# Three groups on each converted weight chunk, and a written engine order from group 3 on

## The chip, the cores and the metric

One core of a Trainium2 chip runs the whole program. The metric is device time in microseconds (us) of one execution. The five engines that matter are TensorE (PE; its weight loads are listed as PEld), VectorE (DVE), ScalarE (ACT), GpSimd (POOL) and SyncE (SP, which issues most DMAs).

## The reference

```python
def reference(q, k, v, moe_w_in, moe_w_out, ...):        # attention -> dense layer -> routed experts
    scores = q @ k.T / sqrt(64); mask 0 <= row - col < 128; bias -slope[h] * |row - col|
    attn = softmax(scores); x = attn @ v                 # 4 x 8 heads x 576 x 64 -> x: 2304 x 512
    h = max(x @ w_in, 0); x = (h * h) @ w_out            # 512 -> 2048 -> 512
    logits = x @ w_gate + log1p(exp(x @ w_noise)) * noise
    top2 of 8 experts, softmax weights of the two
    out = sum over both: weight * (max(x @ w1[e], 0) @ w2[e])    # 512 -> 1024 -> 512
```

The dense weights arrive as float64, everything else as float32.

## The kernel before

The 2304 tokens are 18 **tiles** `i` of 128. Attention is done by tile. The dense layer is done by 9 **groups** `g` of 256 tokens (tiles 2g and 2g+1) and 16 **chunks** `f` of 128 of the 2048 hidden columns. One pair (g, f) is called a **unit** here. Its matmuls are `mm1` (12 matmuls 128x256 into `h`, L128) and `mm2` (6 matmuls 128x512 into the two banks `y` of the group, L133); between them stand the gate steps: three ACT passes (ReLU, square, high part `gh`) and on DVE the low part `gl` (L345). `mm2` comes two units behind its `mm1`. Each value is carried as a high and a low float32r part, which is why there are three products for each.

A tile's attention on PE is: scores (L250, 12 matmuls for each half of the heads), transposes (L290), value products (L305). On DVE it is: `ktl` (L218), the masked merge (L255), bias and row maximum (L264), the small softmax steps (L267, L273, L274), the two masked copies of the transposed weights (L293, L294) and the low part `xl` of its output (L312). ACT does copies and exponentials, POOL the scaling by the row sum (L277) in the later tiles.

A float64 chunk is converted once, in two halves, by `load_w_moe` (L99 to L118): an ACT pass, the sign on POOL (L111), two bit operations and a subtraction on DVE (L112, L114, L117). The result lives in one of 16 slots: chunks 0 to 7 in `ring_a`, chunks 8 to 15 in `ring_b`, whose memory is that of the pool `at0`, the attention buffers of the first tiles. So no chunk from 8 on is finished before the tiles in `at0` are.

**First pass.** `FT = 4` tiles are in `at0`, and groups 0 and 1 share the chunks, group 1 four chunks behind (`LATE = 4`). Group 2 and the later ones then run one after another, all chunks being there. Beside the units of group g (g from 2) the attention of group g+1 is issued in pieces (`a_pair`), and the routing of group g-1 (`routes`: output transposes, gate matmuls L382 and L391, top two, ranks, table matmuls L486). Group 8 has no attention beside it; its units cover the first loads of expert weights, and the routing of group 7. Then come the eight experts.

The Tile scheduler decides the order of all instructions on each engine from the order of the calls, the dependences and its own costs. PSUM has eight banks: four `y`, two `t` (transposes, value products, later scores) and two `h`. The zero fill of the output (`out_dram<-ysb`, 4608 KB) and the constants of the routing (`consts_late`) are issued at the beginning of group 2.

Of the kernel before, what the change touches and what calls it, by code (L numbers as in the profile page):

```python
# [22 lines left out]
def kernel(  # L23
# [75 lines left out]
    def load_w_moe(f):  # L99
        w = slot()  # L100
        for u in range(2):
# [4 lines left out]
            a = s64.tile([P, DM], I32, name="wa", bufs=3)  # L106
# [4 lines left out]
            nc.gpsimd.tensor_scalar(hi.bitcast(F32), hi.bitcast(F32), 0.0, None, op0=OP.mult)  # L111
            nc.vector.scalar_tensor_tensor(out=lo, in0=lo, scalar=29, in1=hi,  # L112
# [44 lines left out]
    def consts_late():  # L157
# [3 lines left out]
        nc.gpsimd.iota(io128, pattern=[[1, P]], base=0, channel_multiplier=0,  # L161
                       allow_small_or_imprecise_dtypes=True)
# [24 lines left out]

    def T(shape, dt=F32):
        return psp.tile(shape, dt, name="t", bufs=2)
# [10 lines left out]
    QT, VT, SB, PT, QK = {}, {}, {}, {}, {}  # L200
# [13 lines left out]
    def a_qk(i, what="qk"):  # L214
        t = QK.pop(i)
# [3 lines left out]
        if "q" in what:  # L219
            qh = A["p"].tile([P, H // 2, P], F32R, name="qh", bufs=A["qt"])  # L220
            ql = A["p"].tile([P, H // 2, P], F32R, name="ql", bufs=A["qt"])
            eng = nc.vector if i < 1 else nc.gpsimd
            eng.tensor_tensor(out=t[:, 0], in0=t[:, 0], in1=qscale[:, :, None].to_broadcast([P, H // 2, P]),
                              op=OP.mult)
            nc.scalar.activation(qh, t[:, 0], AF.Copy)
            eng.tensor_tensor(out=ql, in0=t[:, 0], in1=qh.bitcast(F32), op=OP.subtract)
            QT[i] = (qh, ql)
# [11 lines left out]
    def a_s(i, hf):  # L239
# [4 lines left out]
        sp = [psp.tile([P, 2, 2, P], F32, name="y", bufs=4) if A["early"] else T([P, 2, 2, P]) for _ in range(2)]  # L244
        for pp in range(2):
            p = 2 * hf + pp
            for n, (a, b) in enumerate(((qh, kh), (qh, kl), (ql, kh))):
                for c in range(2):
                    r = slice(64 * c, 64 * c + 64)
                    nc.tensor.matmul(sp[c][:, pp], a[r, p, :], b[r, p, s0:s0 + 2, :], start=(n == 0), stop=(n == 2))  # L250
# [5 lines left out]
        mx = A["p"].tile([P, 4], F32, name="mx", bufs=A["sb"])  # L256
        nb = A["p"].tile([P, 4], F32, name="nb", bufs=A["sb"])
        sm = A["p"].tile([P, 4], F32, name="sm", bufs=A["sb"])
        rs = A["p"].tile([P, 4], F32, name="rs", bufs=A["sb"])
# [7 lines left out]
        nc.vector.tensor_tensor(out=nb, in0=mx, in1=nslope[:, 4 * hf:4 * hf + 4], op=OP.mult)  # L267
        for pp in range(2):
            for c in range(2):
                j = 2 * pp + c  # L270
                nc.scalar.activation(sb[:, c, pp], sb[:, c, pp], AF.Exp, bias=nb[:, j:j + 1],  # L271
                                     scale=2.0 ** -(4 * hf + j + 1), accum_out=sm[:, j:j + 1])
        nc.vector.tensor_scalar(sm, sm, 1e-9, None, op0=OP.add)  # L273
# [23 lines left out]
    def a_av(i, hf):  # L297
        o = T([P, 2, P])
        pts = PT.pop((i, hf))
        vv = (VT[max(i - 1, 0)], VT[i])  # L300
        for pp in range(2):
            for n in range(2):
# [10 lines left out]
        if hf == 1:  # L313
            VT.pop(i - 1, None)
# [547 lines left out]
```

## Time and profile before

| | us |
|---|---|
| median of 3 runs | 1071.94 (1069.54 to 1072.7) |
| profiled execution | 1073.84 (span 1072.1) |
| PE busy | 1014.4 (95%) |
| DVE busy | 569.1 (53%) |
| ACT busy | 507.7 (47%) |
| POOL busy | 245.2 (23%) |
| first mm1 of groups 2, 3 and 8 | 182.46, 247.99, 544.59 |
| first mm1 of expert 0 | 604.15 |

Spans are counted from the start of the profiled execution. The busy share is an average over stages with different limits, so the stages are read one by one. The profile also shows the granted clock of PE in each stretch (1.00 is full).

### The profile page before, as it was taken

The numbers are of one execution on the slowest core, as the hardware profiler recorded it, in microseconds if no ns is written. First come the engines' busy times: TensorE is split into PE (matmuls) and PEld (weight loads), VectorE is DVE, ScalarE is ACT, GpSimd is POOL, SyncE is SP. The second block draws the span as 40 slices with busy tenths as digits, with TensorE's granted clock in tenths as the row PEclk, the third lists the DMA queues.
The fourth block names the chain that finished last, engine by engine and source line by source line (L and its number), as shares of the span: only waits on it lengthen the run. The fifth ranks groups of instructions, "written<-read, shape, count | busy, mean of one in ns | idle before, by whom it ended". The sixth has DMA issues, their size and how long they took to land.

```text
span 1072.1 us, 17953 instructions
## 1 busy us (share of the span) xinstructions
PE 1014.4 (95%) x6636; PEld 876.9 (82%) x6636; DVE 569.1 (53%) x1700; ACT 507.7 (47%) x1272; POOL 245.2 (23%) x219
## 2 busy tenths in 40 slices
PE   4788899899999999999999899999999999999996
PEld 3567788788888888888887787988988888888885
DVE  7989873766555556465537455434443444342312
ACT  5876664665656465565557534332333232321110
POOL 2545530211101021111000012314141412232111
PEclk9989999999999999999999999999999999999998
DMA  6334412611101111110025506535353444432111
GB/s 235 118 126 152 149 59 85 236 31 50 31 30 31 35 46 31 40 41 20 12 91 159 175 27 186 166 113 177 98 164 108 159 124 138 132 105 71 45 46 47
DMA packets 36522, 104.19 MB, mean 97 GB/s; under 512 B 7527, under 2 KB 7783, under 8 KB 36432
## 3 DMA queue, kind: packets, MB, share of 16 engines
q1 hardware_dynamic: 27232, 75.72, 22.1%
q0 software_dynamic: 9200, 27.29, 8.1%
q8 instruction: 53, 0.87, 0.4%
q14 instruction: 37, 0.30, 0.1%
HBM read 86.02 MB, written 20.00 MB: 99 GB/s over the span
## 4 chain that ended last, share of the span: by engine, by line
PE 69%; DVE 9%; DMA 8%; issue 6%; ACT 6%; POOL 1%; SPq 0%; POOLq 0%; ACTq 0%; DVEq 0%
PE h L128 30%; PE y L133 27%; DMA old<-out_dram,idx 4%; PE t L133 3%; PE t L305 3%; PE y L250 2%; PE t L569 1%; PE t L290 1%; DMA qks<-in_qk_dram 1%; ACT sb L271 1%; DMA xg<-yd,idx 1%; DVE gl L345 1%; DVE sb L264 1%; DVE w L112 1%; POOL w L111 1%
## 5 line engine op out<-in xcount | busy, mean ns | idle before, releaser
L128 PE MATMUL h<-xh,w 128*128 128x256 f32 x1152 | 237.7, 289 | 5.3 <-ACT r L342 4.8
L128 PE MATMUL h<-xeh,w 128*128 128x304 f32 (+2 forms) x1024 | 229.5, 305 | 0.9 <-ACT xeh L572 0.9
L128 PEld LDWEIGHTS h<-xh,w 128*128 128x128 f32 x1152 | 190.7, 193 | 15.4 <-ACT r L342 6.6
L133 PE MATMUL y<-w,gh 128*128 128x512 f32 x576 | 189.0, 408 | 0.6 <-ACT gh L344 0.4
L128 PEld LDWEIGHTS h<-xeh,w 128*128 128x128 f32 x1024 | 171.4, 188 | 3.5 <-ACT xeh L572 1.1
L128 PE MATMUL h<-xl,w 128*128 128x256 f32 x576 | 164.8, 286 | 0.0
L96 DVE TENSOR_TENSOR w<-wst,w 128x1024 fp32r<-128x1024 f32 x64 | 78.4, 1226 | 148.5 <-ACT w L95 148.4
L128 PE MATMUL h<-xel,w 128*128 128x304 f32 (+2 forms) x512 | 154.8, 302 | 0.4 <-DVE wt L574 0.4
L133 PE MATMUL y<-w,hh 128*128 128x512 f32 x464 | 145.0, 393 | 0.0
L95 ACT ACTIVATE w<-wst 128x1024 fp32r<-128x1024 f32 x64 | 67.8, 1059 | 134.5 <-PE t L133 128.0
L588 ACT ACTIVATE hh<-h 128x304 fp32r<-128x304 f32 (+1 forms) x120 | 50.4, 420 | 147.6 <-PE h L128 146.1
L133 PE MATMUL y<-w,gl 128*128 128x512 f32 x288 | 114.3, 398 | 2.2 <-DVE gl L345 2.2
L133 PEld LDWEIGHTS y<-w,gh 128*128 128x128 f32 x576 | 99.1, 189 | 20.3 <-ACT r L343 1.0
L342 ACT ACTIVATE r<-h 128x256 f32<-128x256 f32 x144 | 54.4, 378 | 127.9 <-PE h L128 84.0
L128 PEld LDWEIGHTS h<-xl,w 128*128 128x128 f32 x576 | 111.0, 193 | 3.9 <-issue 0.3
L345 DVE TENSOR_TENSOR gl<-r,gh 128x256 fp32r<-128x256 f32 x144 | 66.5, 461 | 83.2 <-ACT gh L344 82.3
L589 DVE SCALAR_TENSOR_TENSOR hl<-h,hh 128x304 fp32r<-128x304 f32 (+1 forms) x120 | 55.9, 466 | 102.5 <-ACT hh L588 102.5
L541 POOL DMA_INDIRECT xg<-yd,idx x40 | 40.7, 1018 | 275.8 <-PE h L128 125.0
L128 PEld LDWEIGHTS h<-xel,w 128*128 128x128 f32 x512 | 96.4, 188 | 1.8 <-DVE wt L574 0.6
L133 PEld LDWEIGHTS y<-w,hh 128*128 128x128 f32 x464 | 83.9, 188 | 14.9
L277 POOL TENSOR_TENSOR sb<-sb,rs 128x512 f32<-128x512 f32 x28 | 29.8, 1064 | 273.9 <-ACT sb L253 130.4
L133 PE MATMUL y<-w,hl 128*128 128x512 f32 x232 | 91.2, 393 | 0.0
(190 smaller groups left out, 1620.9 us busy)
## 6 DMA issues: line engine op xcount, KB each, us to landing
wst<-in_w_exp_dram SPq DMA_DIRECT2D x64, 512.0 KB, 3.7
w<-in_w_moe_dram SPq DMA_DIRECT2D x32, 512.0 KB, 3.7
qks<-in_qk_dram SPq DMA_DIRECT2D x20, 512.0 KB, 3.7
vs<-in_v_dram SPq DMA_DIRECT2D x20, 256.0 KB, 2.7
yd<-ysb SPq DMA_DIRECT2D x18, 256.0 KB, 2.0
out_dram<-ysb SPq DMA_DIRECT2D x1, 4608.0 KB, 14.2
xg<-yd,idx POOLq DMA_INDIRECT x40, 3.7
out_dram<-old,idx POOLq DMA_INDIRECT x29, 2.8
```

The lines of the kernel that those rows point to most:

```text
L95: nc.scalar.activation(w[:, 0], st, AF.Copy)
L96: nc.vector.tensor_tensor(out=w[:, 1], in0=st, in1=w[:, 0].bitcast(F32), op=OP.subtract)
L128: nc.tensor.matmul(ps, w[:, wi, c], x[:, kk, :], start=(n == 0), stop=(n == 3 * KD - 1))
L133: nc.tensor.matmul(ps, g, w[:, wi, DM:], start=(start and n == 0), stop=(stop and n == 2))
L250: nc.tensor.matmul(sp[c][:, pp], a[r, p, :], b[r, p, s0:s0 + 2, :], start=(n == 0), stop=(n == 2))
L277: nc.gpsimd.tensor_tensor(out=sb, in0=sb, in1=r.to_broadcast([P, 2, 2, P]), op=OP.mult)
L305: nc.tensor.matmul(o[64 * c:64 * c + 64, pp, :], vv[n][:, 4 * hf + j, :], pts[n][:, j, :], start=(n == 0), stop=(n == 1))
L342: nc.scalar.activation(r, h, AF.Relu)
L345: nc.vector.tensor_tensor(out=gl, in0=r, in1=gh.bitcast(F32), op=OP.subtract)
L541: nc.gpsimd.indirect_dma_start(out=xg, out_offset=None, in_=yd[:rows, :], in_offset=col(e, t), bounds_check=rows - 1, oob_is_err=False)
L588: nc.scalar.activation(hh[:, c], ps, AF.Relu)
L589: nc.vector.scalar_tensor_tensor(out=hl[:, c], in0=ps, scalar=0.0, in1=hh[:, c].bitcast(F32), op0=OP.max, op1=OP.subtract)
```

## The change

1. First pass: `FT = 6` tiles in `at0`, and **three** groups on each chunk, starting at chunk steps 0, 3 and 6. `mm2` comes two units behind in the common order. Chunk 8 now waits for tile 5. The constants, the zero fill and the attention buffers of tiles 6 and 7 (`at2`) move to step 13; tiles 6 and 7 and the routing of groups 0 and 1 follow in steps 14 to 21.
2. From group 3 to group 7 the engines PE, ACT, DVE and POOL run in **the order of the calls** (`manual_schedule`). Each unit has a place, between its `mm1` and its gate steps, and a table (`a_places`, `r_places`) puts one step of attention or routing there. The scores of a tile are one block of both halves, its value products are one block in one PSUM bank (L339), its output copy is one pass of 512 columns (L352). What is left of the table (`rest`) goes into group 8.
3. PSUM: `t` is gone, and six banks `y` serve everything. `gh` and `gl` get three buffers each.
4. Conversion: the sign on POOL reads the contiguous ACT result `af` and writes a tile `sg` of its own; `wa` has two buffers instead of three.

```diff
-            a = s64.tile([P, DM], I32, name="wa", bufs=3)
+            a = s64.tile([P, DM], I32, name="wa", bufs=2)
+            sg = s64.tile([P, DM], I32, name="wsg", bufs=1)
-            nc.gpsimd.tensor_scalar(hi.bitcast(F32), hi.bitcast(F32), 0.0, None, op0=OP.mult)
-            nc.vector.scalar_tensor_tensor(out=lo, in0=lo, scalar=29, in1=hi,
+            nc.gpsimd.tensor_scalar(sg.bitcast(F32), af, 0.0, None, op0=OP.mult)
+            nc.vector.scalar_tensor_tensor(out=lo, in0=lo, scalar=29, in1=sg,
...
     def T(shape, dt=F32):
-        return psp.tile(shape, dt, name="t", bufs=2)
+        return psp.tile(shape, dt, name="y", bufs=6)
...
+    def a_places(i):
+        return [lambda: a_q1(i), lambda: (a_kq(i), load(i + 1, "qk")), lambda: a_s(i),
+                lambda: (a_cp(i, 0), a_cp(i, 1)), lambda: a_mx(i, 0), lambda: (a_ex(i, 0), a_mx(i, 1)),
+                lambda: (a_nm(i, 0), a_ex(i, 1)), lambda: (a_nm(i, 1), a_tp(i, 0)),
+                lambda: (a_m(i, 0), a_tp(i, 1)), lambda: (a_m(i, 1), a_av(i)), lambda: (a_x(i), load(i + 1, "v"))]
...
-    FT = 2 * GT
-    LATE = 4
-    NA = 3
+    FT = 3 * GT
+    LATE = (0, 3, 6)
+    NA = 6
...
-    for s in range(NFC + LATE):
-        now = [(g, s - LATE * g) for g in range(2) if 0 <= s - LATE * g < NFC]
-        for g, f in now:
-            m_mm1(g, f)
+    for s in range(NFC + LATE[-1]):
+        for g in range(len(LATE)):
+            f = s - LATE[g]
+            if not 0 <= f < NFC:
+                continue
+            m_h(g, f)
+            m_g(g, f)
+            prev.append((g, f))
+            while len(prev) > 2:
+                q = prev.pop(0)
+                m_mm2(*q)
+                if q[1] == NFC - 1:
+                    m_y(q[0])
+                    fill += routes(q[0])
+            for _ in range(2):
+                if s >= NFC and fill:
+                    fill.pop(0)()
...
+        if s + 3 == NFC:
             s64_cm.__exit__(None, None, None)
...
+    with tc.manual_schedule(engines=order):
+        for g in range(len(LATE), NG - 1):
+            for f in range(NFC):
+                m_h(g, f)
+                for fn in places.pop(NFC * g + f, ()):
+                    fn()
+                m_g(g, f)
+                prev.append((g, f))
+                m_mm2(*prev.pop(0))
+    rest = [fn for n in sorted(places) for fn in places[n]]
```

DVE at the end of the pool `at0`, which lets `ring_b` begin. `w`/`wa` are a chunk's buffers, `gl` is a gate's low part, `xl` a tile's output, and `wsg` the new sign tile. Before (tile 4's output comes among later chunks, long after `at0`):

```order
287 L345 TENSOR_TENSOR gl<-r,gh 128x256
288 L114 SCALAR_TENSOR_TENSOR wa<-wa,w_1526 128x512
289 L112 SCALAR_TENSOR_TENSOR w_1636<-w_1636 128x512
290 L117 TENSOR_TENSOR w<-wa,w 128x512
291 L114 SCALAR_TENSOR_TENSOR wa<-wa,w_1636 128x512
292 L312 TENSOR_TENSOR xl<-t,xh 128x2x128
293 L255 COPY_PREDICATED sb<-pmask,t 128x256
```

And of the change (the end of tile 5, and the first conversion into `ring_b` behind it):

```order
280 L325 TENSOR_TENSOR pv<-y,mprev 128x512
281 L326 TENSOR_TENSOR pc<-y,mcur 128x512
282 L385 TENSOR_TENSOR gl<-r,gh 128x256
283 L170 MEMSET ones 128x128
284 L171 MEMSET tab 128x152
285 L161 TENSOR_SCALAR tri<-io_2072 128x128
286 L168 TENSOR_SCALAR idx<-idx 128x16
287 L352 TENSOR_TENSOR xl<-y,xh 128x4x128
288 L118 TENSOR_TENSOR w<-wa,w 128x512 x2
```

Before, 14 chunks were converted when tile 4 ended; now tiles 4 and 5 end ahead of every chunk from 8 on, with 11 gate steps and four operations of the constants ahead of them.

PE in the units of group 3 and after, the value products of a tile. `h` is an mm1's bank, `pv`/`pc` are the masked weights of one half. Before:

```order
1188 L305 MATMUL t_3648<-pc_3576,vs_3324 64x128 x2
1189 L133 MATMUL y_3130<-w_1345,gh_3553 128x512 x2
1190 L133 MATMUL y_3130<-w_1345,gl_3554 128x512
1191 L133 MATMUL y_3131<-w_1345,gh_3553 128x512 x2
1192 L133 MATMUL y_3131<-w_1345,gl_3554 128x512
```

And of the change:

```order
1088 L129 MATMUL h_3250<-xh_2506,w_1021 128x256
1089 L339 MATMUL y_3267<-pv_3222,vs_2510 64x128 x2
1090 L339 MATMUL y_3267<-pc_3223,vs_2820 64x128 x2
1091 L339 MATMUL y_3267<-pv_3222,vs_2510 64x128 x2
1092 L339 MATMUL y_3267<-pc_3223,vs_2820 64x128 x2
1093 L339 MATMUL y_3267<-pv_3263,vs_2510 64x128 x2
1094 L339 MATMUL y_3267<-pc_3264,vs_2820 64x128 x2
1095 L339 MATMUL y_3267<-pv_3263,vs_2510 64x128 x2
1096 L339 MATMUL y_3267<-pc_3264,vs_2820 64x128 x2
1097 L134 MATMUL y_3121<-w_706,gh_3197 128x512 x2
```

The second half (`pv_3263`, `pc_3264`) now follows the first without an mm1 or mm2 between them, into the same bank.

PE at the first scores of tile 6, in the last units of the first pass. Of the change:

```order
743 L134 MATMUL y_699<-w_2042,gl_2247 128x512
744 L129 MATMUL h_2360<-xh_625,w_1844 128x256
745 L258 MATMUL y_2197<-kth_2098,qh_2191 128x256
746 L258 MATMUL y_2197<-ktl_2099,qh_2191 128x256
747 L258 MATMUL y_2197<-kth_2098,ql_2192 128x256
748 L258 MATMUL y_2197<-kth_2098,qh_2191 128x256
749 L258 MATMUL y_2197<-ktl_2099,qh_2191 128x256
750 L258 MATMUL y_2197<-kth_2098,ql_2192 128x256
751 L129 MATMUL h_2360<-xl_626,w_1844 128x256
752 L258 MATMUL y_2198<-kth_2098,qh_2191 128x256
```

Three groups hold all six banks `y`, so these scores come behind group 0's last mm2 (rows up to 743), one bank at a time.

## Rows read from the trace of the kernel before

**Rows 1.** Stages, windows view: stretch, us, busy (count) of PE, PEld, DVE, ACT, POOL; PEclk; DMA share; GB/s.

```profile
0.00:92.80 92.80, 67.04 (x426) 51.49 (x426) 81.03 (x231) 65.52 (x192) 40.08 (x31) 0.94 0.47 160
92.80:182.46 89.66, 81.41 (x531) 70.38 (x531) 63.11 (x139) 56.38 (x149) 34.18 (x25) 0.96 0.33 104
182.46:247.99 65.53, 61.48 (x463) 51.22 (x462) 45.81 (x192) 40.30 (x114) 12.14 (x11) 1.00 0.35 121
247.99:544.59 296.60, 294.88 (x2212) 253.71 (x2211) 164.31 (x687) 174.01 (x518) 40.67 (x37) 1.00 0.12 36
544.59:604.15 59.56, 53.26 (x342) 45.28 (x340) 35.90 (x99) 39.64 (x75) 3.79 (x3) 1.00 0.45 139
```

**Rows 2.** Chain of waits in group 3: start us, us, engine, line, matmuls.

```profile
298.95 1.02 PE t L305 x16
299.98 1.60 PE y L133 x6
...
304.66 1.41 PE h L128 x12
...
306.07 1.40 PE y L133 x6
...
312.01 0.91 PE y L250 x12
312.91 1.59 PE y L133 x6
...
327.92 0.59 PE t L290 x4
```

**Rows 3.** Windows view of line 128 alone: PE and PEld busy (count) up to 92.80.

```profile
0.00:92.80 92.80, 21.89 (x120) 18.40 (x120) 0.94 0.47 160
```

**Rows 4.** The same for DVE lines 117 and 312.

```profile
0.00:92.80 92.80, 10.88 (x16) 0.94 0.47 160
...
0.00:92.80 92.80, 3.26 (x8) 0.94 0.47 160
```

**Rows 5.** Groups by line and form, DVE: busy, mean ns | idle before, releaser.

```profile
L264 DVE CUSTOM_DVE_ANT_0 sb<-sb,relv 128x128 f32<-128x128 f32 x144 | 46.8, 364 | 0.2
...
L264 DVE DVE_READ_ACCUMULATOR2_ANT mx<- 128x1 f32 x144 | 11.5, 80 | 0.0
...
L255 DVE COPY_PREDICATED sb<-pmask,y 128x256 f32<-128x256 int32 x56 | 23.4, 443 | 29.0 <-ACT sb L253 28.7
...
L293 DVE TENSOR_TENSOR pv<-t,mprev 128x512 f32<-128x512 f32 x36 | 24.3, 676 | 4.6 <-PE t L290 4.6
...
L312 DVE TENSOR_TENSOR xl<-t,xh 128x256 fp32r<-128x256 f32 x36 | 14.9, 417 | 4.1 <-ACT xh L311 4.1
...
L218 DVE TENSOR_TENSOR ktl<-qks,kth 128x512 fp32r<-128x512 f32 x20 | 14.8, 739 | 4.4 <-ACT kth L217 4.4
...
L274 DVE RECIPROCAL rs<-sm 128x4 f32<-128x4 f32 x36 | 6.3, 175 | 0.7
...
L345 DVE TENSOR_TENSOR gl<-r,gh 128x256 fp32r<-128x256 f32 x144 | 66.5, 461 | 83.2 <-ACT gh L344 82.3 <-PE y L133 0.3
```

**Rows 6.** The same view, the conversion's steps on DVE.

```profile
L112 DVE SCALAR_TENSOR_TENSOR w<-w 128x512 int32<-128x512 int32 x32 | 29.9, 935 | 5.4 <-POOL w L111 5.0
...
L114 DVE SCALAR_TENSOR_TENSOR wa<-wa,w 128x512 int32<-128x512 int32 x32 | 23.9, 758 | 0.5 <-ACT xh L311 0.5
...
L117 DVE TENSOR_TENSOR w<-wa,w 128x512 fp32r<-128x512 f32 x32 | 23.0, 730 | 0.1
```

**Rows 7.** DMA issues: us from issue to landing last.

```profile
qks<-in_qk_dram SPq DMA_DIRECT2D x20, 512.0 KB, 3.7
...
out_dram<-ysb SPq DMA_DIRECT2D x1, 4608.0 KB, 14.2
```

**Rows 8.** Groups by line and form, POOL: busy, mean ns | idle before.

```profile
L111 POOL TENSOR_SCALAR w<-w 128x512 f32<-128x512 f32 x32 | 55.6, 1743 | 55.9 <-ACT wa L110 48.2 <-DVE sb L255 2.9 <-issue 1.8
...
L277 POOL TENSOR_TENSOR sb<-sb,rs 128x512 f32<-128x512 f32 x28 | 29.8, 1064 | 273.9 <-ACT sb L253 130.4 <-DVE g_d L411 68.0 <-DVE rs L274 56.3
```

**Rows 9.** Waits of PE in group 8: us in total, times, longest.

```profile
PE t L569 <- issue: 3.3, 1, 3.3
PE t L486 <- DVE r_b L482: 1.4, 1, 1.4
```

More of the change, by code (lines that the diff above doesn't have):

```diff
@@ L242, in a_s, with a_cp @@
         s0 = min(kslot(i), kslot(i - 1))
-        cur, old = kslot(i) - s0, kslot(i - 1) - s0
[L244 to L250, printed above, removed]
+        for hf in hfs:
+            sp = [T([P, 2, 2, P]) for _ in range(2)]
+            for pp in range(2):
+                p = 2 * hf + pp
+                for n, (a, b) in enumerate(((qh, kh), (qh, kl), (ql, kh))):
+                    for c in range(2):
+                        r = slice(64 * c, 64 * c + 64)
+                        nc.tensor.matmul(sp[c][:, pp], a[r, p, :], b[r, p, s0:s0 + 2, :],
+                                         start=(n == 0), stop=(n == 2))
+            SP[i, hf] = sp
+    def a_cp(i, hf):
+        sp = SP.pop((i, hf))
+        s0 = min(kslot(i), kslot(i - 1))
+        cur, old = kslot(i) - s0, kslot(i - 1) - s0
         sb = A["p"].tile([P, 2, 2, P], F32, name="sb", bufs=A["sb"])
@@ L351, in m_mm2 @@
         if f == 0:
-            YP[g] = [psp.tile([P, DM], F32, name="y", bufs=4) for t in range(GT)]
+            YP[g] = [T([P, DM]) for t in range(GT)]
         gh, gl = GG.pop((g, f))
@@ L596, in e_mm2 @@
             for t in tiles:
-                YE[e, t] = psp.tile([P, DM], F32, name="y", bufs=4) if t < 4 else T([P, DM])
+                YE[e, t] = T([P, DM])
         for t in tiles:
@@ L666 @@
             gp = gp_cm.__enter__()
-    fill = routes(0) + routes(1)
-    early = False
-    for g in range(2, NG):
-        last = g + 1 == NG
-        if g == 2:
-            A["cm"].__exit__(None, None, None)
             late = ctx.enter_context(tc.tile_pool(name="late", bufs=1, side="right", reuse_waits="tile"))
@@ new lines, with place @@
+            i = FT + 2
+            afill2 += a_places(i)[:2]
+        if s + 2 >= NFC:
+            for fn in afill2[2 * (s + 2 - NFC):2 * (s + 3 - NFC)]:
+                fn()
+    a_s(FT + 2)
+    while fill:
+        fill.pop(0)()
+    early = False
+    places = {}
+    def place(n, fn):
+        places.setdefault(n, []).append(fn)
+    for g in range(len(LATE), NG - 1):
+        n = NFC * g
+        for t in range(GT):
+            i = (g + 1) * GT + t
+            for j, fn in enumerate(a_places(i)):
+                if j > 2 or i > FT + 2:
+                    place(n - 3 + NFC // GT * t + j, fn)
+        for j, fn in r_places(g - 1).items():
+            place(n + j, fn)
@@ new lines @@
+    A["cm"].__exit__(None, None, None)
+    m2 = ctx.enter_context(tc.tile_pool(name="m2", bufs=1, side="right"))
+    fill = []
+    g = NG - 1
+    for f in range(NFC):
+        m_h(g, f)
+        m_g(g, f)
+        prev.append((g, f))
+        while len(prev) > 2:
+            q = prev.pop(0)
+            m_mm2(*q)
+            if q[1] == NFC - 1:
+                m_y(q[0])
+                fill += routes(q[0])
+        if rest:
+            rest.pop(0)()
+        if f >= 2:
+            loads_to(min(f - 1, NEC))
+        if fill:
+            fill.pop(0)()
+            if not fill and not early:
+                fill = [g_early] + [lambda t=t: e_gather(0, t) for t in range(AT)] + \
+                    [lambda t=t: e_tx(0, t) for t in range(AT)]
+                early = True
@@ L716, in overflow @@
+    for q in prev:
+        m_mm2(*q)
+    m_y(g)
+    fill += routes(g)
     def overflow():
```

266 lines of the change are left out of this document (146 added, 120 removed).

## The prediction

> **What bounds the kernel now.** I read the stages first, in the windows view [rows 1]: in each, the engine with the highest busy share is the one to ask. Up to 92.80 us (the end of tile 3, and of the pool `at0`) DVE is busy 81.03 of 92.80 and PE 67.04: DVE bounds. Between 92.80 and 247.99 (the rest of the shared chunks, group 2) PE is busy 81.41 + 61.48 = 142.9 of 155.2, DVE 108.9: PE bounds, with gaps. In groups 3 to 7 PE is busy 294.88 of 296.60: it bounds, and only 1.7 us are idle. In group 8 it idles 6.3 us.
>
> Then I priced PE's work from the chain of waits [rows 2]. A unit is 1.41 (mm1) + 1.40 (mm2) = 2.81 us. A tile's attention is scores 2 x 0.91, products 2 x 1.02 and transposes 2 x 0.59, 5.0 us; behind scores or products the next mm2 takes 1.59 or 1.60, so 0.2 more than 1.40. Two to four such places a tile add 0.4 to 0.8, so I take 5.5 a tile. Groups 3 to 7 take 296.6 / 5 = 59.3 each: 16 x 2.81 = 45.0, two tiles 11.0, and 3.3 left for routing and its switches. There is hardly any wait in this stage that a better order could remove.
>
> The same bill for 92.80 to 247.99: 10 units were done before it (120 of the 12-matmul blocks [rows 3]), so 38 of the 48 of groups 0 to 2 remain: 106.8; four tiles 22.0; routing of two groups 6.6; together 135.4 of 155.2. So **19.8 us were lost there**, and this is what three groups on a chunk could win back: a chunk gives 3 x 2.81 = 8.4 us of PE work where two groups gave 5.6, while its conversion costs DVE 2 x (0.935 + 0.758 + 0.730) = 4.8 us [rows 6].
>
> **The change, part by part.**
>
> *A longer DVE-bound head.* Chunk 8 needs the memory of `at0`, which now holds six tiles. By 92.80 before, four tiles and eight chunks were through DVE (8 and 16 instructions, [rows 4]). The order of the change has the same eight chunks (16 subtractions) ahead of tile 5's end, so what is added is two tiles. A tile on DVE, from [rows 5]: 8 x (0.364 + 0.080) + 4 x 0.443 + 4 x 0.676 + 2 x 0.417 + 0.739 + 6 x 0.17 = 10.6 us, the last term for the small softmax steps. Two tiles 21.2, three more `gl` 1.4, one half chunk's two bit operations 1.7, four operations of the constants 1.0 (small ones, at 0.17 to 0.3): 25.3 us. With no idle DVE time added tile 5 ends at 92.8 + 25.3 = 118.1; at the stage's busy share of 0.87 it is 122. Below, if half of the old stage's 11.8 idle us are filled, 112; above, with some waits for ACT and POOL between the steps, 124. I take **118**, since the steps of two more tiles can fill each other's gaps, but the last tile's chain can't be shortened.
>
> *From there to group 3.* Before tile 5's end 11 units' mm1 stand in PE's order, so 37 follow: 104.0. Tiles 6 and 7: 11.0. The scores of tile 8, which now come ahead of group 3: 1.8. Tile 6's split scores (the order shows them behind group 0's last mm2, one bank at a time): 0.7, bounded by 0 and two extra switches of each kind, 1.0. Routing of two groups: 6.6. Together 124.1. Then waits. Before, 19.8 were lost in a stretch whose first part was bound by DVE; now a chunk needs 4.8 + 3 x 0.46 = 6.2 us of DVE for 8.4 us of PE, so PE should seldom wait for chunks. Towards the end DVE has tiles 6 and 7 (21.2), two routings and the gates in some 15 units. I take 6 (bounds 3 and 14). Group 3 begins at 118 + 124.1 + 6 = **248**, where it began at 247.99. So I expect the head's loss and the shared stretch's gain to cancel: 0, with bounds of -11 and +14.
>
> *The zero fill* moves ahead of the loads of tiles 6 and 7 on SP's queue. It takes 14.2 us and such a load 3.7 [rows 7], so 17.9, and the order leaves some 7 units, 19.7 us, between them and their use. Hidden; if the cover is gone, up to 6 us come on top.
>
> *Groups 3 to 7.* The units and the matmuls are the same. Merged blocks remove one switch at the scores and one at the products of each tile, 0.2 each: 0.4 x 10 = 4.0. Tile 8's scores have moved ahead: 1.8. Nothing else can be saved: 1.7 us of idle time is all there is [rows 1]. What the written order can do is add waits; I take none, since each place has a whole unit of 2.81 us, and mm2 is two units behind its gates. -5.8 (bounds -7.5 and +4).
>
> *Group 8 and after.* What is left of the table, the ranks and tables of group 6, moves into the first units of group 8: 0.6 on PE, and some 6 us on DVE ahead of the routing of group 7, on whose end the first expert gathers wait. PE waits 3.3 us at those transposes and 1.4 at the tables today [rows 9]. I take 1.0 more (bounds 0 and 4), 1.6 with the 0.6. The experts are untouched: 0.
>
> *The sign on POOL.* The line takes 1743 ns with its strided input, and a contiguous pass of 128x512 took 1064 ns [rows 8]; DVE waited 5.0 us for it in all [rows 6]. The pass now reads ACT's result, for which POOL waited already (48.2 us in rows 8), so it can't start later. Gain between 0 and 5.0 on DVE; most of that lies in the old gaps, so 0. The Trainium skill ("GPSIMD Engine Reference", Performance pitfalls for Q7 kernels) says that a read costs more only where the step between elements is over 8 bytes. The old step is 8 bytes, so by that rule the pass would not get shorter at all; by the rows it could lose up to 0.68 us of 1.74. Both leave the sum as it is.
>
> **The sum.** 0 - 5.8 + 1.6 = -4.2 us. The profiled execution of before took 1073.84 (span 1072.1), 1.9 above the median of the runs, 1071.94. So the profile of the change should show some 1069.6, and the median **1067.7**. A measurement of this kernel can tell about 0.3% from no change, 3.2 us: faster is below 1068.7, slower above 1075.2. The forecast stands just on the faster side.
>
> **The rivals.**
>
> *The head shrinks.* Tile 5 ends at 112, and PE is then never short of work: waits 3 instead of 6. Group 3 begins at 112 + 124.1 + 3 = 239, -9; groups -5.8, group 8 +0.6: -14, a median of **1058**. For it: 19.8 lost us to win, and 11.8 idle us on DVE in the head. Against it: the head's DVE work is serial at its end, with nothing but attention left.
>
> *DVE stays the bound, and the head's loss isn't paid back* (the other side). Two tiles' attention, 21.2 us of DVE, goes ahead of chunk 8, and PE has only 11 units to do meanwhile. If tile 5 ends at 124 and the shared stretch loses 14, group 3 begins at 124 + 124.1 + 14 = 262, +14; with -5.8 and +1.6, +10: a median of **1082**. It decides from the point at which the head costs over 7.4 us, that is if group 3 begins after 255.4. For it: with both routings and two tiles DVE holds about three quarters of this stretch, `r` has one buffer, and all y banks are taken until group 0 ends. Against it: 8.4 us of PE work a chunk against 6.2 of DVE.
>
> *The written order waits.* The scheduler's order left PE 1.7 us idle in 296.6; a fixed place can come too early for what it needs. If two places in each of the ten tiles wait 0.4 us, that is +8: in all +3.8, a median of **1076**. For it: a step late in its place holds up the next mm1 on PE and the next gate on ACT and DVE, in order. Against it: the gates have two units of slack.
>
> **How the numbers follow.** The forecast has 0.48: its own range is 1060 to 1075, 0.25 of it below 1068.7 and 0.23 within 0.3%. The shorter head 0.22, all faster. The head not paid back 0.20, slower. The waiting order 0.10, 0.04 within 0.3% and 0.06 slower. Faster 0.47, same 0.27, slower 0.26. The range reaches from below the shorter head's 1058 by the other half of its bound (1051) to just above the rival on the other side (1083).
>
> **What would show it.** In the profile after: tile 5's output pass (L352) ends near 118 (right between 114 and 122); group 3's first mm1 is near 248; groups 3 to 7 take about 58.1 each, with PE idle for 2 us in all; mm2 behind a tile's scores is slow once a tile instead of twice; group 8 begins near 538 and the first expert near 600. If group 3 begins before 243 or after 255 the head was priced wrongly. If a group takes over 59.3, the order waits, and the waits of PE name the place. If the loads of tile 6 end a wait on POOL or PE, the zero fill lost its cover.

## The result, and the profile after

The change is **slower**: 1083.39 us (median of 4 runs, 1078.9 to 1084.01) against 1071.38 for the kernel before on the same chip (4 runs), a ratio of 1.0104 with a 95% interval of 1.0072 to 1.0136. Forecast was 1067.7, and the range ended at 1083. The profiled execution took 1078.90 (span 1077.1), the shortest of the four; the other three took 4 to 5 us more, at a mean granted clock of PE of 0.967 to 0.980 instead of 0.986. The profiles show 5.0 us of the loss (spans 1077.1 and 1072.1): the change's lies 4.5 us below its median of 1083.39, and the one of before (1073.84) 2.5 us above 1071.38.

The windows view of the change, at the places that answer to [rows 1] (tile 5's end, first mm1 of group 3, of group 4, of group 8, of expert 0; columns as there):

```profile
0.00:125.20 125.20, 91.46 (x587) 66.40 (x588) 95.99 (x293) 82.81 (x256) 42.23 (x37) 0.92 0.40 128
125.20:261.70 136.50, 127.60 (x826) 107.28 (x826) 77.55 (x212) 80.59 (x200) 33.51 (x24) 0.97 0.35 113
261.70:324.30 62.60, 59.94 (x467) 52.70 (x466) 37.27 (x163) 39.49 (x112) 8.76 (x8) 1.00 0.12 35
324.30:552.30 228.00, 228.00 (x1746) 203.46 (x1745) 135.59 (x537) 138.64 (x402) 33.47 (x30) 1.00 0.12 37
552.30:608.20 55.90, 53.63 (x346) 45.53 (x344) 38.43 (x121) 39.33 (x74) 3.73 (x3) 1.00 0.46 148
608.20:1077.10 468.90, 456.69 (x2671) 405.01 (x2671) 180.41 (x359) 133.33 (x228) 115.14 (x112) 1.00 0.36 113
```

Group 3 begins at 261.7 where it began at 247.99: **+13.7**. Groups 3 to 7 take 62.6 + 228.0 = 290.6 instead of 296.6: **-6.0**. Group 8 takes 55.9 instead of 59.6 (-3.7), the experts 468.9 instead of 468.0. The sum is +5.0. So groups 3 to 7 took the time that was forecast; the first pass lost more than twice what they won.

In the head (up to tile 5's end) DVE is busy 95.99 of 125.2, a share of 0.77, where it had 0.87 up to 92.80 [rows 1]. **DVE has become less of a bound, and the head is longer all the same**: it waits, 29.2 us in all, where it was idle for 11.8 up to 92.80. Two waits of DVE (us in total, times, longest), up to 92.80 before, and up to 125.2 in the change:

```profile
DVE pv L293 <- PE t L290: 3.0, 3, 1.9
...
DVE w L112 <- POOL w L111: 0.8, 2, 0.4
```

```profile
DVE pv L325 <- PE y L318: 12.4, 6, 3.8
DVE w L113 <- POOL wsg L112: 5.1, 5, 1.9
```

The largest wait of the head is that of the masked copies (`pv`) for the transposes on PE, and PE itself waits 19.0 us there for ACT's scaling by the row sum (L307), which stands ahead of the transposes. One such wait, of 2.37 us, ends at 62.99: four transposes stand on PE among the value products of another tile, in a stretch at 1.2 GHz (half the clock):

```profile
57.30:64.00 6.70, 5.40 (x24) 2.90 (x24) 4.33 (x10) 4.43 (x11) 2.50 (x2) 0.50 0.49 159
```

Behind tile 5's end (125.2 to 261.7) the two largest waits of DVE are:

```profile
DVE gl L385 <- ACT gh L384: 19.7, 14, 2.4
DVE w L113 <- POOL wsg L112: 13.1, 14, 1.7
```

So DVE waits 18.2 us for the sign on POOL in all, where it was 5.0 before [rows 6], and most of that lies behind the head. The group of that pass on POOL (busy, mean ns, idle before it and what ended it), and a piece of the chain of waits in the shared stretch (start us, us):

```profile
L112 POOL TENSOR_SCALAR wsg<-wa 128x512 f32<-128x512 f32 x32 | 51.3, 1602 | 79.1 <-ACT wa L111 67.4 <-DVE w L113 7.6 <-DVE nb L283 3.2
```

```profile
150.62 1.51 POOL wsg L112
152.13 0.02 issue
152.15 0.04 DVE w L113
152.19 0.57 issue
152.76 0.70 DVE w L118
153.46 0.02 issue
153.48 0.68 ACT wa L111
154.16 0.07 issue
154.24 1.51 POOL wsg L112
```

One half chunk goes round ACT, POOL and DVE in 154.24 - 150.62 = 3.62 us. In this piece the ring closes over the two `wa`: ACT's pass for the next half (L111) waits for L118 of an earlier one, and L118 stands in DVE's order behind the L113 that waits for POOL. ACT waits so 15.2 us up to group 3; POOL waits for the one `wsg` (L113) 7.6 us.

In the head PE idles early, and its clock is lower. The windows view from 40 to 60 and 60 to 80 us, of the kernel before and then of the change:

```profile
40.00:60.00 20.00, 17.60 (x114) 13.37 (x110) 18.66 (x52) 16.89 (x52) 8.18 (x6) 0.91 0.43 134
60.00:80.00 20.00, 17.47 (x101) 12.73 (x103) 18.07 (x48) 15.00 (x45) 9.65 (x7) 0.83 0.34 110
```

```profile
40.00:60.00 20.00, 10.38 (x73) 7.93 (x70) 17.42 (x50) 15.15 (x46) 8.00 (x5) 0.83 0.46 133
60.00:80.00 20.00, 17.43 (x92) 11.74 (x92) 14.93 (x44) 12.30 (x41) 7.52 (x5) 0.74 0.29 91
```

From 40 to 60 us PE is busy 10.38 of 20 us, where it had 17.60; in the next 20 us the mean clock is 0.74 of full speed instead of 0.83, that is, part of that time at 1.2 GHz instead of 2.4. How much of the longer head the clock makes, no run separates.

### The profile page after: what moved, and what is told of

It reads as the page before. It is cut to its first block, busy times and chain, and to the rows that moved or that the text cites. A ratio compares the mean times of both kernels' runs of the same rounds, so it can differ in the third digit from the quotient of the medians.

```text
span 1077.1 us, 17898 instructions
## 1 busy us (share of the span) xinstructions
PE 1017.3 (94%) x6636; PEld 880.4 (82%) x6636; DVE 565.2 (52%) x1681; ACT 514.2 (48%) x1269; POOL 236.8 (22%) x214
## 4 chain that ended last, share of the span: by engine, by line
PE 71%; DVE 8%; DMA 7%; issue 5%; ACT 5%; POOL 3%; SPq 0%; POOLq 0%; ACTq 0%; DVEq 0%
PE y L134 30%; PE h L129 30%; DMA old<-out_dram,idx 4%; PE y L339 3%; PE y L258 3%; POOL wsg L112 2%; DMA wst<-in_w_exp_dram 2%; PE y L318 2%; PE y L653 1%; ACT sb L292 1%; DVE sb L280 1%; DVE w L118 1%; DVE w L96 1%; DVE w L113 1%; ACT wa L111 1%
## 5 line engine op out<-in xcount | busy, mean ns | idle before, releaser
L129 PE MATMUL h<-xh,w 128*128 128x256 f32 x1152 | 234.4, 285 | 3.3 <-ACT r L382 1.6
L129 PEld LDWEIGHTS h<-xh,w 128*128 128x128 f32 x1152 | 188.4, 190 | 13.3 <-ACT r L382 2.3
L134 PE MATMUL y<-w,hh 128*96 128x512 f32 (+1 forms) x592 | 185.0, 394 | 0.0
L385 DVE TENSOR_TENSOR gl<-r,gh 128x256 fp32r<-128x256 f32 x144 | 71.5, 496 | 128.8 <-ACT gh L384 128.6
L95 ACT ACTIVATE w<-wst 128x1024 fp32r<-128x1024 f32 x64 | 67.8, 1060 | 136.1 <-PE y L134 115.7
L134 PEld LDWEIGHTS y<-w,hh 128*96 128x96 f32 (+1 forms) x592 | 104.5, 182 | 22.1
L134 PE MATMUL y<-w,hl 128*96 128x512 f32 (+1 forms) x296 | 116.4, 393 | 0.0
L673 DVE SCALAR_TENSOR_TENSOR hl<-h,hh 128x304 fp32r<-128x304 f32 (+1 forms) x120 | 55.9, 466 | 103.3 <-ACT hh L672 95.5
L302 POOL TENSOR_TENSOR sb<-sb,rs 128x512 f32<-128x512 f32 x24 | 25.1, 1045 | 229.6 <-DVE rs L299 195.2
```

The costliest lines, as they stand in the source:

```text
L95: nc.scalar.activation(w[:, 0], st, AF.Copy)
L129: nc.tensor.matmul(ps, w[:, wi, c], x[:, kk, :], start=(n == 0), stop=(n == 3 * KD - 1))
L134: nc.tensor.matmul(ps, g, w[:, wi, DM:], start=(start and n == 0), stop=(stop and n == 2))
L302: nc.gpsimd.tensor_tensor(out=sb, in0=sb, in1=r.to_broadcast([P, 2, 2, P]), op=OP.mult)
L385: nc.vector.tensor_tensor(out=gl, in0=r, in1=gh.bitcast(F32), op=OP.subtract)
L673: nc.vector.scalar_tensor_tensor(out=hl[:, c], in0=ps, scalar=0.0, in1=hh[:, c].bitcast(F32), op0=OP.max, op1=OP.subtract)
```

## The experiments

Times of the profiled executions, in us from the start; ratios against the kernel before on the same chip, over all executions of both. "Tile 5" is the end of its output copy; the columns behind it are first mm1s. These times come from one execution each, and they move without an edit: the head of the change stands in the same order on DVE, ACT and POOL in `e3`, `e12` and `e13`, and there tile 5 ends between 125.2 and 127.5; that of `e11` stands again in `e15` (120.9 and 122.8), and the first pass of `e10` in `e14` (group 3 at 252.1 and 256.6). So 2 us in the head, or 4 at group 3, prove nothing by themselves.

| run | ratio (95%) | tile 5 | group 3 | group 4 | group 8 |
|---|---|---|---|---|---|
| before | 1 | | 248.0 | 307.5 | 544.6 |
| change | 1.0104 (1.0072 to 1.0136) | 125.2 | 261.7 | 324.3 | 552.3 |
| e1_conv_before | 1.0066 (1.0038 to 1.0094) | 123.0 | 257.0 | 319.6 | 547.6 |
| e2_before_conv_after | 1.0027 (0.9999 to 1.0056) | | 249.7 | 309.3 | 546.5 |
| e3_scheduler | 1.0138 (1.0094 to 1.0182) | 125.7 | 262.2 | 327.5 | 560.5 |
| e4_two_groups | 1.0157 (1.0125 to 1.0188) | | 277.4 | 334.9 | 562.8 |
| e5_halves | 1.0095 (1.0069 to 1.0121) | 126.0 | 261.4 | 326.3 | 554.3 |
| e8_late9 | 1.0120 (1.0084 to 1.0156) | 130.7 | 274.7 | 331.6 | 559.6 |
| e8b_late410 | 1.0108 (1.0077 to 1.0138) | 131.8 | 275.0 | 331.8 | 559.8 |
| e9_combo | 1.0019 (1.0001 to 1.0037) | 119.8 | 259.8 | 316.6 | 544.6 |
| e10_front_before | 0.9997 (0.9975 to 1.0018) | | 252.1 | 309.1 | 542.1 |
| e11_conv_halves | 1.0029 (1.0009 to 1.0049) | 120.9 | 255.1 | 320.0 | 548.0 |
| e12_no_rank01 | 1.0008 (0.9984 to 1.0031) | 127.5 | 258.7 | 315.6 | 543.6 |
| e13_interleave | 1.0084 (1.0052 to 1.0117) | 125.7 | 259.4 | 321.9 | 549.9 |
| e14_three_buffers | **0.9942** (0.9924 to 0.9960) | | 256.6 | 313.5 | 541.4 |
| e15_route1_placed | 0.9996 (0.9976 to 1.0015) | 122.8 | 256.8 | 316.4 | 544.3 |

### The conversion, undone and done alone

In the change (`e1_conv_before`), and the reverse in the kernel before (`e2_before_conv_after`):

```diff
-            a = s64.tile([P, DM], I32, name="wa", bufs=2)
-            sg = s64.tile([P, DM], I32, name="wsg", bufs=1)
+            a = s64.tile([P, DM], I32, name="wa", bufs=3)
-            nc.gpsimd.tensor_scalar(sg.bitcast(F32), af, 0.0, None, op0=OP.mult)
+            nc.gpsimd.tensor_scalar(hi.bitcast(F32), hi.bitcast(F32), 0.0, None, op0=OP.mult)
-            ... scalar=29, in1=sg,
+            ... scalar=29, in1=hi,
```

> The change with the conversion of before (three buffers wa, the sign in place on the high words), all else as in the change. Ring theory: in the change, two wa buffers and one sign tile make the conversion a ring ACT, POOL, DVE of 3.6 us a half chunk, and the gate steps behind it on DVE wait. Without it the shared units 20 to 27 take 2.8 to 3.0 us instead of 3.6 (8 units, -6 us) and tile 5 ends some 4 us earlier: group 3 begins near 251, time 1068 to 1075. Head theory: six tiles ahead of chunk 8 are too much whatever the conversion does: tile 5 still ends at 122 to 126, group 3 begins after 256, time 1078 or more.

> The kernel before with the conversion of the change alone. Ring theory: the same ring of 3.6 us a half chunk appears in chunks 8 to 15, group 2 begins 4 to 8 us later than 182.5, time 1075 to 1080. Head theory: the conversion has slack in the first pass, time within 3 us of 1071.

Measured: undone in the change, 1079.34 us, ratio 1.0066 instead of 1.0104 (the intervals overlap); tile 5 ends 2.2 us earlier, group 3 begins 4.7 earlier. By the marks set beforehand this is the head theory's outcome: tile 5 at 123.0, group 3 at 257.0, more than 1078 us. Units 20 to 27 took 25.4 us, 3.2 each (27.9 in the change), and the stretch from tile 5's end to the unit at which tile 6's scores begin (unit 39) took 83.9 us (123.0 to 206.9) against 84.9 (125.2 to 210.1). In `e11` and `e15`, which have the same old conversion, units 20 to 27 took 27.8 and 27.7 again, and the stretch 84.9 and 85.1. So **the ring of 3.6 us is in the chain there, but taking it away saves 1 us at most: another wait stands behind it**. Done alone in the kernel before, the new conversion costs 1.7 us up to group 3, and its ratio of 1.0027 (1076.45 us) can't be told from no change: group 2 begins at 183.8, not 4 to 8 us later than 182.5.

### The written order, and two groups instead of three

```diff
-    with tc.manual_schedule(engines=order):
+    with contextlib.nullcontext():
```

> The change without the written order: the calls are the same, the scheduler decides the order in groups 3 to 7. If the merged blocks are what shortened groups 3 to 7 (290.6 us in the change, 296.6 before), they stay at 290 to 293 and the time within 3 us of the change. If the written order was, they go back to 296, +6 on the change.

Measured: 1090.10 us. Up to group 3 nothing changes; groups 4 to 7 take 560.5 - 327.5 = 233.0 instead of 228.0 (group 3 took 65.3 instead of 62.6, but 65 in `e5` and `e11` too, with the written order). The blocks are still whole in PE's order, so **the merged blocks alone don't bring the 57.4 us a group; the written order does, given the blocks and the three gate buffers**. The chain of waits of this run in group 5 shows what the scheduler's order loses:

```profile
420.56 0.94 DVE g_u L455
...
425.26 1.02 DVE g_nl L464
426.28 0.02 issue
426.30 0.97 DVE g_nl L465
...
427.81 0.43 DVE gl L386
428.24 0.04 issue
428.28 1.20 PE y L135 x4
```

DVE takes routing in one go, the gate's `gl` comes behind it, and `mm2` waits for that. In the written order of the change the chain of group 5 is PE from end to end, also where this routing stands. A piece of it, with both merged blocks:

```profile
401.81 1.42 PE h L129 x12
403.23 1.90 PE y L339 x32
405.13 1.60 PE y L134 x6
406.73 1.43 PE h L129 x12
408.17 1.62 PE y L258 x24
409.79 1.59 PE y L134 x6
```

Then two groups on a chunk, all else as in the change:

```diff
-    FT = 3 * GT
-    LATE = (0, 3, 6)
-    NA = 6
+    FT = 2 * GT
+    LATE = (0, 4)
+    NA = 3
-            for fn in afill2[2 * (s + 2 - NFC):2 * (s + 3 - NFC)]:
+            for fn in afill2[3 * (s + 2 - NFC):3 * (s + 3 - NFC)]:
```

> The change with two groups a chunk, as before (four tiles in the first pool, group 1 four chunks behind; written order from group 2, tiles 4 and 5 issued in steps 14 to 19). Head theory: chunk 8 begins near 95, and the loss up to group 3 shrinks to 5 or less: 1066 to 1075. Ring theory: chunks 8 to 15 still take 7.2 us each, and two groups have only 5.6 us of PE work for each, so the loss stays or grows: 1080 or more.

Measured: 1090.55 us, a miss for the head theory and not for the reason that the ring theory gave: chunk 15 was done by 156.5, the last shared mm1 began at 172.6, and then PE was busy 23.55 of 42.9 us until group 2 began at 215.5, since tiles 4 and 5 stand in the last steps behind the zero fill (tile 4's load ends at 175.6). It says that **the third group is what covers the late tiles**; it doesn't compare the two first passes. One thing the ring theory had right: from 86.7 to 137.4 the sign passes begin 3.6 us apart, 7.2 us a chunk, and units 8 to 17 take 3.6 us each.

### The first tiles' outputs, and the distance of the groups

`e5_halves`, in tiles 0 to 5 only:

```diff
-                lambda: (a_tp(i, 0), a_m(i, 0)), lambda: (a_tp(i, 1), a_m(i, 1)), lambda: (a_av(i), a_x(i))]
+                lambda: (a_tp(i, 0), a_m(i, 0)),
+                lambda: (a_av(i, (0,)), a_x(i, (0,)), a_tp(i, 1), a_m(i, 1)), lambda: (a_av(i, (1,)), a_x(i, (1,)))]
...
```

> The change, but in tiles 0 to 5 the value products and the output copy go half by half, as before (the first half's products stand ahead of the second half's transposes). Merge theory: the merged output holds back the first tiles (tile 0 ended at 41.5 us in the change, 36.9 before; tile 3 at 88.3 against 81.7; first mm1 at 44.3 against 35.6), so tile 5 ends 5 to 7 us earlier, near 119, and the time falls by as much, to 1077 or so. Head theory: two more tiles are the whole loss, tile 5 stays at 123 to 126, and the time within 2 us of the change's.

Measured: 1083.58 us. The first tiles do come earlier (tile 0 at 35.5, first mm1 at 35.7), but tile 3 ends at 91.6 and tile 5 at 126.0. That is the head theory's outcome: alone it wins nothing.

`e8_late9` and `e8b_late410`: `LATE = (0, 3, 9)` and `(0, 4, 10)`.

> The change with group 2 nine chunks behind instead of six. Bank theory: tiles 6 and 7 can't start their scores before group 0 gives up its two banks, and then have only the 8 units from 210 us on beside them, so some 9 us of PE are lost there; with three more units behind group 0's end (8.4 us) most of that is won: group 3 5 to 8 us earlier, time 1076 or so. Chunk theory: the shared stretch is bound by chunks or by DVE's total, and two groups a chunk for longer only move the wait: within 3 us of the change, or slower.

> The change with group 1 four and group 2 ten chunks behind. Bank theory: five more units behind group 0's end, so the loss after it is gone (9 us) unless chunks then bind: 1074 to 1078. Chunk theory: 1082 or more, with PE waiting between 125 and 175 us.

Measured: 1087.27 and 1088.76 us. With fewer units early PE idles more in the head (the mean clock from 80 to 100 us is 0.66 and 0.57, in the change 0.91) and tile 5 ends 5.5 and 6.6 us later. And behind group 0's end PE's order still has 8 units beside tiles 6 and 7 (207.3 to 258.2 in the first run); the units that were added stand behind them. So the bank theory isn't tested by this; what it proposed as a cure is none.

`e9_combo` has the conversion of before, the halves, and `LATE = (0, 3, 9)`; `e11_conv_halves` the first two alone.

> Three edits together: conversion of before, halves in tiles 0 to 5, group 2 nine chunks behind. If the three causes are separate they add: 4 + 6 + 6 less than the change, some 1067 to 1070, and level with or below before. If one wait stands behind them all, no more than the best of the three alone.

> The change with two edits: conversion of before, and outputs half by half in tiles 0 to 5 (three groups at 0, 3, 6 as in the change). Alone they moved tile 5's end from 125.2 to 123.0 and 126.0. If they only help together, as in the run with three edits (tile 5 at 119.8), tile 5 ends at 118 to 121 and group 3 begins near 253: time 1074 to 1077. If nine chunks' distance was what helped there, tile 5 stays at 122 or later and the time at 1079 or more.

Measured: 1075.04 and 1075.02 us, ratios 1.0019 and 1.0029. **The two edits together take some 0.75 points off the ratio of the change (1.0104), and the intervals don't overlap**; the third adds nothing that can be told. So the three don't add up as in the first forecast, but they do better than the best of them alone (1079.34). Tile 5 ends at 120.9, and at 122.8 in `e15` with the same head, against 125.2 to 127.5 with the head of the change; whether the old conversion alone (123.0) does as much isn't settled. PE is no busier in that head (85.7 of 120.9 us), but DVE's wait for the transposes is 9.1 us instead of 12.4 and that for POOL 3.4 instead of 5.1. In `e11` group 3 comes 6.6 us earlier than in the change. But behind 205.8 nothing is won, as the windows view of the first mm1 of unit 39 up to group 4 shows for the change and for this run:

```profile
210.10:324.30 114.20, 108.97 (x803) 92.21 (x802) 70.71 (x297) 68.77 (x196) 16.55 (x15) 0.97 0.14 43
```

```profile
205.80:320.00 114.20, 109.09 (x803) 91.83 (x803) 71.20 (x297) 68.54 (x196) 16.62 (x15) 0.97 0.14 43
```

### What is lost behind group 0's end

`e12_no_rank01` leaves out ranks and tables of groups 0 and 1; `e13_interleave` takes the steps of tiles 6 and 7 in turns:

```diff
-        return ty + lg + [lambda: None, rk] + tb
+        return ty + lg + ([lambda: None, rk] + tb if g > 1 else [])
```

```diff
-                afill2 += p
+                afill2.append(p)
+            p, r = afill2
+            afill2 = [*p[:3], r[0], p[3], r[1], p[4], r[2], p[5], *r[3:]]
```

> The change without the ranks and the tables of groups 0 and 1 (this part of the routing is left out, so their tokens reach no expert; only the time up to group 3 is read). If the chains of routing on DVE are what PE waits for behind 210 us (8 us of the chain of waits there), group 3 begins 8 us or more earlier, before 254. If tiles 6 and 7's own chains are, it begins 2 to 4 us earlier, by the work left out.

> The change with the steps of tiles 6 and 7 interleaved instead of one tile after the other. If the loss behind 210 us is the length of two tiles' chains in a row (24 and 27 us), the two overlap and group 3 begins 6 to 9 us earlier, time 1075 to 1078. If the units, DVE or the routing bind there, less than 3 us.

Measured: interleaving moves group 3 by 2.3 us and group 4 by 2.4: less than 3 us, so the tiles' own chains are the lesser part. Without ranks and tables the same stretch takes 103.2 us instead of 114.2:

```profile
212.40:315.60 103.20, 102.10 (x792) 87.59 (x790) 59.03 (x247) 67.80 (x196) 16.65 (x15) 1.00 0.15 47
```

11 fewer records on PE, but 11.7 us less work on DVE, 50 instructions of it in chains of small steps. By the marks that were set this is the second answer, 2 to 4 us and the tiles' own chains: group 3 begins at 258.7, 3.0 us earlier than in the change (5.3 counted from unit 39 on). But the mark stood too early, for the rest shows in group 3 itself, which takes 56.9 instead of 62.6. In the chain of waits of the change such a chain looks like this:

```profile
233.77 0.19 DVE r_ro L514
...
234.82 0.18 DVE r_ri L524
235.02 0.18 DVE r_ri L525
235.22 0.18 DVE r_ri L526
235.43 0.17 DVE r_rf L527
235.60 0.41 DVE gl L385
...
236.42 0.28 DVE r_b L538
...
236.74 0.30 PE y L546
```

This run leaves out work, so `e15_route1_placed` keeps it whole: `e11_conv_halves`, with the routing of group 1 taken out of the first pass and spread over the places of group 3.

```diff
-                    fill += routes(q[0])
+                    fill += routes(q[0]) if q[0] == 0 else []
...
+    r1 = [(0, lambda: (g_ty(1, 0), g_ty(1, 1))), ...
+          (9, lambda: g_rank(1)), (10, lambda: g_rankc(1)), (11, lambda: g_taba(1, 0)), ...
+    for j, fn in r1:
+        place(NFC * len(LATE) + j, fn)
```

> The change with the conversion of before, halves in tiles 0 to 5, and the routing of group 1 spread over the places of group 3, one step a chunk, instead of all steps ahead of group 3. If the squeezed chains of routing are what is still lost behind 206 us (leaving ranks and tables of groups 0 and 1 out gained 8.7 us up to group 4, 2.8 of it work), group 4 begins 5 to 7 us earlier than the 320.0 of the run with the two edits alone, time 1068 to 1071. If tiles 6 and 7 hold PE there, group 4 stays near 319, time 1074 or more.

Measured: 1073.15 us, ratio 0.9996, level with before. Group 4 begins 3.6 us earlier than in `e11`, less than forecast, behind a head that ended 1.9 later. The stretch from unit 39 to group 4 takes 108.5 us with all its work, 5.7 less (112.7 to 115.0 in the change, `e1`, `e5` and `e11`):

```profile
207.90:316.40 108.50, 105.14 (x804) 89.83 (x803) 72.23 (x297) 68.52 (x196) 16.63 (x15) 1.00 0.15 45
```

**So 4 to 6 us of the loss were two groups' routing squeezed into the last units of the first pass.** They show in group 3 (59.5 us here, 64.9 in `e11`), whose first gates stand on DVE behind that routing: in the change the chain of waits runs through its small steps from 262.2 to 268.9 us, and group 3's second mm1 begins 8.4 us behind its first. Here the chain is PE alone from the first mm1 on.

### The old first pass with the written order

`e10_front_before`: two groups, four tiles in `at0`, tiles 4 to 7 and the routing spread as before, outputs by halves and the old conversion; from group 3 on the change. For memory `gh` and `gl` are taken as before from two buffers and, in every third chunk, from a third one in another pool.

```diff
-        gh = m1.tile([P, G], F32R, name="gh", bufs=3)
-        gl = m1.tile([P, G], F32R, name="gl", bufs=3)
+        pool, n = (m1, 2) if g < 2 or f % 3 else (gp, 1)
+        gh = pool.tile([P, G], F32R, name="gh", bufs=n)
+        gl = pool.tile([P, G], F32R, name="gl", bufs=n)
```

> The first pass of before (two groups a chunk, four tiles in the first pool, tiles 4 to 7 spread over steps 4 to 17 and group 2, outputs half by half, conversion of before), and from group 3 on the written order of the change with its merged blocks and six shared banks. If the whole loss lies in the new first pass and the written order is worth what groups 4 to 7 show (57.4 us against 59.5), group 3 begins near 250 (tile 8's scores are ahead of it), and expert 0 some 8 to 10 us before 604: time 1060 to 1065, faster than both kernels. If the shared banks or the new code of the pieces cost something by themselves, group 3 begins after 255 and the time is 1070 or more.

Measured: 1071.88 us, ratio 0.9997. Group 3 begins at 252.1, group 4 at 309.1 (before 307.5, but here tile 10's scores are already done by then), near what was hoped; but groups 4 to 6 take 58.7 each, not 57.4, and the time misses the 1060 to 1065. The waits of ACT in groups 4 to 7 name a buffer:

```profile
ACT r L384 <- PE h L128: 45.5, 23, 2.4
ACT gh L386 <- PE y L133: 13.5, 4, 3.4
```

Four waits of up to 3.4 us, one in each group: chunk 15 of a group and chunk 0 of the next are both multiples of three, so both take the one buffer in the other pool. `e14_three_buffers` counts through:

```diff
-        pool, n = (m1, 2) if g < 2 or f % 3 else (gp, 1)
+        pool, n = (m1, 2) if g < 2 or (NFC * g + f) % 3 else (gp, 1)
```

> The previous run with the first pass of before and the written order, with one edit: from group 2 on gh and gl take turns in three buffers over the group's boundary too (there the last chunk of a group and the first of the next shared one buffer). In that run groups 4 to 7 took 58.7 us, in the change 57.4. If the buffers were the difference, the groups go to 57.4, 5 us in all, time 1066 to 1068 and faster than both kernels. If it is something else (fewer waits left over from group 3), they stay at 58.7 and the time at 1072.

Measured: **1067.55 us** (6 runs, 1066.78 to 1070.46) against 1073.01, ratio 0.9942: **faster than both kernels**, as forecast. That wait is gone, and groups 4 to 6 take 57.4:

```profile
256.60:313.50 56.90, 56.90 (x438) 50.89 (x438) 28.87 (x114) 35.85 (x104) 8.74 (x8) 1.00 0.12 38
313.50:541.40 227.90, 227.90 (x1745) 203.39 (x1744) 135.47 (x537) 138.54 (x402) 33.44 (x30) 1.00 0.12 37
```

This run has the late part of the change and not its first pass (nor its conversion and merged outputs in the first tiles). So the loss of the change lies in these, 0.9942 against 1.0104.

## Why the prediction was wrong

*The head.* This is the step that failed first: "With no idle DVE time added tile 5 ends at 92.8 + 25.3 = 118.1", and I took 118. It ended at 125.2. The sum was too high in work and too low in waits: DVE was busy 96.0 us up to there, where the sum had 81.0 + 25.3 = 106.3, and it was idle for 29.2, where the sum kept the old 11.8. What failed is that DVE was taken as the bound of a stage to which the change also added waits: "the steps of two more tiles can fill each other's gaps" didn't come. The largest of the waits is for the transposes on PE, 12.4 us against 3.0. I also priced the sign on POOL by the duration of its pass (gain 0 to 5.0) and didn't ask what the buffers did, one `wsg` and two `wa` instead of three: DVE's wait for it rose to 5.1 us in the head, and from 5.0 to 18.2 in all. With the old conversion and half outputs together tile 5 ends at 120.9 and 122.8, some 4 us earlier on average; the other 3 or 4 us of the miss are not settled. In one point the ground was wrong too: 92.80 is the end of chunk 7; tile 3 had ended at 81.7, so the 81.0 us held some work of a fifth tile already.

*The shared stretch.* "I take 6 (bounds 3 and 14)" for waits up to group 3. By the same bill 12.4 were lost (136.5 - 124.1), inside the bounds, so the term was mis-sized by 6. Half of the 12.4 were lost up to unit 39 (84.9 us for 28 units, 78.7 at 2.81) and half behind it. I had argued from throughput (6.2 us of DVE for 8.4 of PE a chunk); but gates and conversions share DVE's and ACT's order, and a conversion that waits for POOL holds up the gate behind it. That this is what cost the first half is read from the waits and not shown by a run: undoing the new conversion won 1 us there at most. At the end I counted the routing of two groups as 6.6 us of PE work and not as chains of small DVE steps (some 25 for each group's ranks and tables alone) that must pass one after another within 8 units. Leaving these out won 5.3 us up to group 3. A part of them fell into group 3, which took 62.6 where the next took 57.4; spreading one group's routing won 4 to 6 us there.

*Groups 3 to 7.* Forecast -5.8, measured -6.0. The size was right by luck, for the reasons were not: two errors cancel, a gain in groups 4 to 7 that was larger than forecast and a loss in group 3 (62.6 instead of 59.5). "There is hardly any wait in this stage that a better order could remove" was read from PE's busy time, 294.88 of 296.60 [rows 1]. PE's ends are modelled, and its busy time holds more than work. Groups 4 to 6 have the same matmuls in both kernels (1328 and 1327 records), and they took 178.5 us before and 172.3 in the change:

```profile
307.49:485.97 178.48, 177.19 (x1328) 152.25 (x1327) 98.72 (x412) 105.11 (x312) 26.38 (x24) 1.00 0.12 37
```

```profile
324.30:496.64 172.34, 172.34 (x1327) 153.74 (x1326) 103.15 (x406) 105.63 (x306) 26.83 (x24) 1.00 0.12 38
```

PE counts as busy for nearly all of it both times; the weight loads (PEld), nearly equal in us, fill 0.85 of the one and 0.89 of the other. With group 7 it is 237.1 and 228.0, but there the change does one tile's scores (1.8) less, since tile 10's already stand in group 3. Merged blocks were estimated at 0.8 a group; the scheduler's order with merged blocks and three buffers took 59.1 a group (0.4 less than before), the written order with the shared buffer 58.7, and with three 57.4.

*Group 8.* Forecast +1.6, measured -3.7. In the runs above it took 55.6 to 58.9 us whatever the edit, even with the order of before (56.6); it isn't told apart here.

*The zero fill.* Right: tile 6's last load-fed step was done before PE could use it. On POOL's timeline of the change:

```profile
195.70 1.30 POOL L233 TENSOR_TENSOR ql<-qks,qh 128x512 fp32r<-128x512 f32 x1 [0.74 <-ACT qh L232]
```

The scores begin at 210.4 us, behind group 0's last mm2, as the order showed. With two groups (`e4_two_groups`) that cover is gone and the tile's load is in the chain of waits, for 11.5 us up to 175.6.

*The sign on POOL.* The pass became a little shorter, a median of 1498 ns instead of 1626, far from the 1064 of the other row [rows 8], which is another operation. The Trainium skill ("GPSIMD Engine Reference", Performance pitfalls for Q7 kernels) names a cost only for steps of over 8 bytes; the old step was 8, and the trace agrees to within that 8%, in which the new output tile has a part that no run separates. So packing was no reason to expect much, and DVE's waits for the pass grew.

*The rivals.* The rival on the other side put group 3 at 262 and the median at 1082; measured were 261.7 and 1083.39. It was right in the place, in the size of the head and of the shared stretch, and in its decision point (group 3 after 255.4). Its mechanism, DVE as the bound, was not: DVE's share fell. And that its median came so near is luck: its sum was +10, the profiles show +5.0, and the rest lies in how the profiled executions stand to their medians. The waiting written order (1076) didn't come: groups 4 to 6 take 57.4 us each, below the 59.3 that was its sign; group 3, at 62.6, is over it, but for the routing that was left to it.

*Profile and median.* I carried the sum from one execution to the median by a fixed 1.9 us. The profiled execution of the change was the best of four, 4.5 us below the median. Its mean clock was the highest of the four, but in the nine executions of `e1` time and clock don't go together (1078.26 us at 0.971, 1081.62 at 0.985), so the clock isn't shown to be the reason. With the two edits of `e11` the ratio fell by 0.75 points, some 8 us, while the profiles of the two differ by 4.3 us at group 4.

**What stays open.** With the two edits and the spread routing group 4 still begins at 316.4, 8.9 us later than before, of which 1.8 are tile 10's scores, done by then. How much of the rest is the longer head itself, and how much the shared stretch (84 to 85 us in every variant with three groups at this distance, whatever the conversion), no run here separates. Nor is it shown which edit would take DVE's wait for the transposes out of the head.

## What to carry to other kernels

Before you count a stage as bound by an engine, ask what the change does to the buffers between the engines: one tile fewer in a chain over three engines can turn throughput into latency. An engine that was the bound can show a lower busy share in a longer stage: add up its waits in that stage alone, since a total over the whole run can name a wait that lies elsewhere. A PE busy share of 99% is no proof that nothing waits; compare the time of equal work with another order of it. Marks in a profile move by some us from one execution to the next; find two runs with the same order before you read a small difference. And chains of small steps (routing, softmax) are not priced by their work: give each step a place with a whole unit of other work around it, and look for buffers that meet at a loop's boundary.

## What the runs showed of the hardware

From 60 to 80 us the mean granted clock was 0.74 behind a stretch with PE busy 10.38 of 20 us, and one mm2 block there took 2.47 us instead of 1.40. The clock differs between executions with the same order on the other engines: in that stretch it was 0.94 in `e11` and 0.76 in `e15`, and from 20 to 40 us 1.00 in the change and 0.57 in `e3`. And the sign pass on POOL hardly cares whether its input of 128x512 is strided by 8 bytes: a median of 1498 against 1626 ns.
